# Ten units' second-chunk scores in two column halves, visits to TensorE held open, small VectorE work on ScalarE, and a scheduler with a search

## The chip, the cores and the metric

One Trainium2 chip, one core of it. The metric is the time on the device in microseconds (us) of one execution, as the median of several. Engines are named as in the profile: PE is TensorE (PEld its weight loads), DVE VectorE, ACT ScalarE, POOL GpSimd, SP the engine whose queue issues the DMAs.

## What is computed

A gated linear attention over 4 batches of 8 heads, 768 steps and head size 48, followed by a feed-forward part over all 3072 tokens (384 to 2048 to 384):

```python
scale = np.minimum(mag, 0.999) / (mag + 1e-06)        # mag = |a_re + i a_im|
for t in range(S):
    new_re = ar * S_re - ai * S_im
    new_im = ar * S_im + ai * S_re
    S_re, S_im = new_re + k[t] v[t]^T, new_im
    y[:, :, t] = q[t] . S_re
...
h = x @ w_in                                          # x: y of all heads of a token
g = np.where(h >= 1, h, np.where(h <= -1, 0, (h + 1) ** 2 / 4))
out = g @ w_out
```

All inputs and outputs are fp32.

## The kernel before

**Units.** The work is cut into 12 units `u` of 256 tokens (two chunks `c` of 128), two units side by side in a block; six blocks of 512 tokens go through the feed-forward part. While block `n` is in the feed-forward part, the units of block `n + 1` go through `gates` and `attend`.

**`gates(u)`** loads the gate inputs (`ai`), takes logarithms and angles on ACT, makes running sums of both (units 0 and 1 by matmuls with a triangle, tiles `dec` and `turns`; the others by scans on DVE), rounds the angles to whole turns, and multiplies key and query (`kq`) by growth, cosine and sine on DVE. `spread` moves the products by DMA into head layout, tiles `hd`, 96 rows (real and imaginary of 48) a head.

**`attend(u)`** does for each chunk: `scores` (`sc`: for each of 8 heads a 128 x 128 matrix of keys by queries in fp32, in two groups of four heads, each in one PSUM bank; DVE multiplies it by the causal mask into `am`), `transposes` (`tp`: keys, copied by ACT into `kT`), `values` (`yp`: the state `st` times the queries, plus the masked scores times `V`; ACT copies it to `xr`) and `products` (`dp`: keys by values, which DVE adds to `st`). `values` and `products` use 64 columns of weights at a time and write partitions 0 to 63 and 64 to 127 in turn: here they are called narrow, and scores, transposes and the feed-forward matmuls full. Three PSUM banks `at0` to `at2` are handed round for all of these.

A **visit** is a list of parts that go to PE one behind the other:

```python
if before:                        # values and products of the chunk before
    visit(before + sc[:1])
    visit(sc[1:] + tp)
```

**`moe(blk)`** takes the block through `h` (first product) and `o` (second), each as three float32r matmuls of 512 columns (a high part and a low part of each factor). Between them ACT and DVE make `s`, `g`, `gh`, `gl`. `weights` splits the two weight matrices into high and low parts on DVE and ACT once, in the time of the first block; for the first five it uses PE (`rest`) for the low part.

**The order.** Nothing stands in the order of the code. Each piece is recorded as an operation of a `Plan` with engine, cost in ns, reads, writes and perhaps a due time. `order` works dues backwards through the readers (costs of ACT and DVE times `INFLATE`), then lets each engine in turn take the ready operation with the earliest due. All instructions are emitted in the order of the planned starts, so that each engine's queue follows the plan and only semaphores hold it. A visit's next part was taken at once only if it was ready when the one before was placed; otherwise feed-forward matmuls could come between. `emit` puts idle matmuls (`idle`) where the plan has gaps on PE before the feed-forward part starts.

At the end the flags `fsum`, `fdec`, `wsum` are read, which say whether the fast way holds for these inputs.

Of the kernel before, what the change touches and what calls it, by code (L numbers as in the profile page):

```python
# [28 lines left out]
CH = 128  # L29
U = 256  # L30
# [54 lines left out]
SPLIT_DUE = 3000  # L85

# [38 lines left out]
class Plan:  # L125
# [3 lines left out]
    def __init__(self):  # L129
        self.ops = []  # L130
        self.slots = {}
        self.glued = {}
        self.loose = set()

# [5 lines left out]
    def op(self, eng, cost, fn, r=(), w=(), due=None, dma=0, after=(), glue=None, late=0):  # L140
        i = len(self.ops)
        pre = set(after)
# [26 lines left out]
    def order(self):  # L169
        ops = self.ops  # L170
        n = len(ops)
        succ = [[] for _ in range(n)]
        for i, o in enumerate(ops):
            for p in o[3]:
                succ[p].append(i)
        due = [0.0] * n
        big = 1e12
        for i in range(n - 1, -1, -1):
            eng, cost, _, _, d, dma, late = ops[i]
            t = big if d is None else d  # L180
# [4 lines left out]
            for s in succ[i]:  # L185
                t = min(t, due[s] - own)
            due[i] = t
        left = [len(o[3]) for o in ops]
        ready = [0.0] * n
        end = [0.0] * n  # L190
        start = [0.0] * n
        free = {e: 0.0 for e in ("PE", "DVE", "ACT", "SP", "POOL")}
# [3 lines left out]

        def enable(i):
            heapq.heappush(wait[ops[i][0]], (ready[i], i))

        for i in range(n):  # L200
            if not left[i]:
                enable(i)
        done = 0
        taken = set()
        forced = []
        while done < n:
# [4 lines left out]
            else:  # L211
                best = None
                for e in free:
                    while avail[e] and avail[e][0][1] in taken:
# [9 lines left out]
                    if best is None or t < best[0]:  # L224
                        best = (t, e)
                t, e = best
                while wait[e] and wait[e][0][0] <= t:
# [21 lines left out]
            start[i] = t  # L249
            free[e] = t + cost  # L250
# [10 lines left out]
            for s in succ[i]:  # L261
                left[s] -= 1
                lat = LAT[eng]
                if dma or s in self.loose:
                    lat = 0
                elif ops[s][0] == eng:
                    lat = SAME[eng]
                ready[s] = max(ready[s], end[i] + lat)
                if not left[s]:
                    enable(s)  # L270
            nxt = self.glued.get(i)
            if nxt is not None and not left[nxt]:
                forced.append(nxt)
        self.start, self.end, self.due = start, end, due
        return sorted(range(n), key=lambda i: (start[i], i))
# [46 lines left out]
def gated_scan_moe(  # L322
# [17 lines left out]
    for i, c in enumerate(consts):  # L340
        nc.gpsimd.memset(cst[:, i : i + 1], c)
    c_eps, c_pi2, c_half, c_tiny, c_tin, zero, c_one, c_top = (
# [14 lines left out]

    pl = Plan()
# [5 lines left out]
    def tl(slot, shape, dtype, name, space=None):  # L364
        return pl.tile(
# [203 lines left out]
    def gates(u):  # L569
# [109 lines left out]
        if by_token:  # L679
            D_ = running(A, a, ("o0", "o1"), "dec")  # L680
            for (j0, j1), R in zip(js, D_):
                ve(
                    80,
                    lambda j0=j0, j1=j1, R=R: V_.tensor_copy(
                        state[:, b % 2, 0, j0:j1], R.get()[:, :, U - 1]
                    ),
                    [R],
                    [(STATE[0], j0)],
# [12 lines left out]
        else:  # L701
# [18 lines left out]
            ve(80, lambda: V_.tensor_copy(dst, X0()[:, :, U - 1]), [x0], [STATE[0]])  # L720
# [11 lines left out]
        if by_token:  # L732
            for (j0, j1), R in zip(js, running(I, i, TOKEN[u], "turns")):
                ints = lambda j0=j0, j1=j1: I()[:, j0:j1].bitcast(I32)
                ve(
                    dve((j1 - j0) * U),
                    lambda ints=ints, R=R: V_.tensor_scalar(
                        ints(), R.get(), c, None, op0=ALU.mult
                    ),
                    [R],  # L740
                    [i],
# [41 lines left out]
        if not last:  # L783
            ve(
                80,
                lambda: V_.tensor_scalar_mul(
                    state[:, b % 2, 1], A()[:, :, U - 1], 2 * math.pi
                ),
                [a],
                [STATE[1]],  # L790
# [15 lines left out]
        if u == 1:  # L806
            vt[u] = guest(
                ("o", 4), "V_1", lambda t: t[:, : NC * DM].rearrange("p (c n) -> p c n", c=NC)
            )
        else:  # L810
            vt[u] = tl("V0", [P, NC, DM], F32, f"V_{u}")
        dma(P * NC * DM * 4, lambda t=vt[u]: t.get(), lambda: v[place], w=[vt[u]], late=LATE if u > 1 else 0, eng=LOADS if u > 1 else "SP")
# [100 lines left out]
    def attend(u):  # L913
# [25 lines left out]
        def transposes(c):  # L939
            cs = slice(c * CH, (c + 1) * CH)  # L940
            out = []
            for g in range(2):
# [18 lines left out]
                out.append((4 * 83, run, [hd[h // 3] for h in GROUPS[g]], TP, tail))  # L961
# [3 lines left out]
        def products(c):  # L965
# [4 lines left out]
            ST = tl(turn_of(f"st{b % 2}", 2), [HR, NH, D], F32, f"st_{u}_{c}")  # L970
            carry[b] = ST

            def run():
                for i in range(NH):
                    for a in (0, 64):
# [4 lines left out]
                            V_c[0].get()[:, V_c[1], i * D : (i + 1) * D],  # L980
# [4 lines left out]
            def tail():  # L985
                if old is None:
                    fn = lambda: V_.tensor_copy(ST.get(), DP.get()[:HR])
                else:
                    fn = lambda: V_.tensor_tensor(ST.get(), old.get(), DP.get()[:HR], op=ALU.add)
                pl.op("DVE", dve(DM), fn, r=[DP] + ([old] if old else []), w=[ST])  # L990

            return [(NH * 124, run, [*kT, V_c[0]], DP, tail)]

        def scores(c):
            cs = slice(c * CH, (c + 1) * CH)
            out, ams = [], []
            for g in range(2):
# [649 lines left out]
```

## Time and profile before

| what | value |
|---|---|
| median of 3 runs | 579.27 us (579.22 to 580.12) |
| the profiled execution's own time | 578.85 us |
| its span in the profile | 577.1 us |
| granted TensorE clock | 0.996 |
| PE busy, PEld busy | 562.0, 475.9 us |
| DVE busy, ACT busy | 431.9, 406.9 us |

The span is that of the instructions; 1.75 us of the execution lie around it. Busy times of PE come from modelled ends, and a fp32 matmul shows as two records. Rows in order of time have start and length in us, engine, line, operation, tile written and tiles read, and the number of merged instructions; in brackets the idle time before and what ended it. Rows of groups have busy time, mean ns of one and idle time before. Rows of stretches have, after the stretch and its length, PE, PEld, DVE, ACT and POOL busy us (and counts), the granted clock, the DMA engines' share and GB/s.

### The profile page before, as it was taken

To read this page: it belongs to the slowest core of one execution; us is meant where nothing else is said; L and a number is where in the kernel's file an instruction comes from. 1 tells how busy PE (TensorE), PEld (TensorE's weight loads), DVE (VectorE), ACT (ScalarE), POOL (GpSimd) and SP (SyncE) were. 2 spreads that over 40 slices of the span, in tenths; PEclk is the share of its full clock that TensorE was granted. 3 is DMA by queue.
4 is the path that set the end of the run, shared out by engine and by line. 5 is a ranking of instruction groups with operands and counts; after the bars stand their busy time and mean duration, and the time that the engine had idled before them with its cause. 6 is when DMAs were issued, how large, how long until landed. Compare 5 with 4: busy or idle time off the path is not lost.

```text
span 577.1 us, 9921 instructions
## 1 busy us (share of the span) xinstructions
PE 562.0 (97%) x3888; PEld 475.9 (82%) x3888; DVE 431.9 (75%) x625; ACT 406.9 (71%) x660; POOL 3.3 (1%) x29
## 2 busy tenths in 40 slices
PE   7999999989999999999999999999999999999994
PEld 7788988878888888888888888888888888888883
DVE  4998999989879588579489879788885544455552
ACT  7787899877899998985476666657652333379972
POOL 2000000000000000000000000000000000000000
PEclk9999999999999999999999999999999999999998
DMA  8677443773751623722601612503312200078801
GB/s 352 249 202 253 129 159 109 212 263 121 184 169 43 187 81 111 227 80 73 177 6 40 215 56 82 172 1 90 111 56 72 72 1 8 20 286 292 308 25 61
DMA packets 23142, 77.20 MB, mean 134 GB/s; under 512 B 4336, under 2 KB 9904, under 8 KB 23088
## 3 DMA queue, kind: packets, MB, share of 16 engines
q1 hardware_dynamic: 23088, 76.50, 41.1%
q8 instruction: 32, 0.52, 0.4%
q14 instruction: 22, 0.18, 0.1%
HBM read 51.90 MB, written 4.72 MB: 98 GB/s over the span
## 4 chain that ended last, share of the span: by engine, by line
PE 73%; DVE 12%; ACT 8%; DMA 3%; issue 2%; SPq 0%; ACTq 0%; DVEq 0%
PE o L1302 28%; PE h L1227 28%; PE sc L1004 6%; PE yp L1053 3%; PE yp L1045 3%; DMA raw_o<-in_wl_dram 2%; PE dp L977 2%; ACT ai L608 2%; PE tp L948 2%; ACT x L608 1%; PE px L1138 1%; DMA ai<-in_art_dram 1%; DVE kq L725 1%; DVE kq L834 1%; ACT s L1262 1%
## 5 line engine op out<-in xcount | busy, mean ns | idle before, releaser
L1227 PE MATMUL h<-xH,wi 128*128 128x512 f32 x576 | 180.4, 394 | 0.0
L1302 PE MATMUL o<-gh,wo 128*128 128x512 f32 x576 | 180.1, 394 | 0.0
L1302 PEld LDWEIGHTS o<-gh,wo 128*128 128x128 f32 x576 | 106.3, 188 | 21.8 <-issue 0.7
L1227 PEld LDWEIGHTS h<-xH,wi 128*128 128x128 f32 x576 | 106.1, 188 | 21.1
L1302 PE MATMUL o<-gl,wo 128*128 128x512 f32 x288 | 112.4, 390 | 0.2 <-DVE gl L1289 0.2
L1227 PE MATMUL h<-xL,wi 128*128 128x512 f32 x288 | 112.5, 391 | 0.0
L1271 DVE TENSOR_TENSOR g<-h,s 128x512 f32<-128x512 f32 x96 | 65.8, 685 | 61.0 <-ACT s L1252 42.3
L1252 ACT ACTIVATE s<-h,cst 128x512 f32<-128x512 f32 x96 | 65.6, 685 | 40.4 <-PE h L1227 36.1
L1289 DVE TENSOR_TENSOR gl<-g,gh 128x512 fp32r<-128x512 f32 x96 | 65.9, 687 | 34.5 <-ACT gh L1285 34.4
L1285 ACT CAST gh<-g 128x512 fp32r<-128x512 f32 x96 | 59.1, 615 | 44.6 <-DVE g L1279 44.0
L1302 PEld LDWEIGHTS o<-gl,wo 128*128 128x128 f32 x288 | 54.1, 188 | 12.2 <-DVE gl L1289 0.6
L1227 PEld LDWEIGHTS h<-xL,wi 128*128 128x128 f32 x288 | 54.0, 188 | 12.1 <-DVE xL L1204 0.4
L608 ACT ACTIVATE ai<-ai 128x768 f32<-128x768 f32 x49 | 41.2, 843 | 19.6 <-DVE ai L777 9.2
L1004 PE MATMUL sc<-hd 96*128 96x128 f32 x384 | 49.9, 278 | 0.1
L1004 PEld LDWEIGHTS sc<-hd 96*128 96x128 f32 x384 | 47.1, 191 | 2.8 <-ACT xr L1065 0.5
L1279 DVE SCALAR_TENSOR_TENSOR g<-s,g 128x512 f32<-128x512 f32 x64 | 44.2, 690 | 1.8
L1053 PE MATMUL yp<-am,V 128*64 128x128 f32 x384 | 35.5, 273 | 0.1
L1012 DVE TENSOR_TENSOR am<-sc,sums 128x512 f32<-128x512 f32 x48 | 32.5, 683 | 3.1 <-PE sc L1004 2.9
L1045 PE MATMUL yp<-hd,st 96*64 96x128 f32 x320 | 32.1, 278 | 1.7 <-DVE am L1012 1.6
L402 ACT ACT_TABLE_LOAD x21 | 26.9, 1283 | 0.4
L1045 PEld LDWEIGHTS yp<-hd,st 96*64 96x64 f32 x320 | 19.1, 135 | 8.7 <-issue 4.3
L1053 PEld LDWEIGHTS yp<-am,V 128*64 128x64 f32 x384 | 23.6, 136 | 1.6 <-DVE am L1012 0.5
(111 smaller groups left out, 673.5 us busy)
## 6 DMA issues: line engine op xcount, KB each, us to landing
chk<-in_wl_dram SPq DMA_DIRECT2D x16, 768.0 KB, 5.9
kq<-in_kq_dram SPq DMA_DIRECT2D x12, 768.0 KB, 4.9
ai<-in_ari_dram SPq DMA_DIRECT2D x10, 768.0 KB, 6.5
hd<-x SPq DMA_DIRECT2D x24, 288.0 KB, 4.2
hd<-kq SPq DMA_DIRECT2D x24, 288.0 KB, 5.4
raw_i<-in_wl_dram SPq DMA_DIRECT2D x8, 768.0 KB, 5.6
raw_o<-in_wl_dram SPq DMA_DIRECT2D x8, 768.0 KB, 6.7
V<-in_v_dram SPq DMA_DIRECT2D x12, 384.0 KB, 3.2
```

Source lines behind the costliest of these rows:

```text
L608: lambda: A_.activation(out(), src(), f, **kw),
L1004: PE_.matmul(SC.get()[:, i, :], t[:, 0, cs], t[:, 1, cs], start=True, stop=True)
L1012: lambda: V_.tensor_tensor(AM.get(), SC.get(), mask.unsqueeze(1).to_broadcast([P, 4, CH]), op=ALU.mult,),
L1045: PE_.matmul(o_, st.get().rearrange("p h e -> p (h e)")[:, lo : lo + 64], head(h)[:, 1, cs], start=True, stop=False,)
L1053: PE_.matmul(o_, V.get()[:, c, lo : lo + 64], ams[pr // 2].get()[:, 2 * (pr % 2) + e, :], start=st is None, stop=True,)
L1227: PE_.matmul(H.get(), weight["i", f // 2].get()[:, f % 2, part, sl], x.get()[:, j, :], start=j == 0 and n == 0, stop=j == NJ - 1 and n == 2,)
L1252: lambda: A_.activation(SS.get(), H.get(), AF.Relu, bias=c_half, scale=-0.5 if spare else 0.5),
L1271: lambda: V_.tensor_tensor(G.get(), H.get(), SS.get(), op=ALU.max),
L1279: lambda: V_.scalar_tensor_tensor(G.get(), SS.get(), 1.0, G.get(), op0=ALU.min, op1=ALU.mult),
L1285: pl.op("ACT", act(T), lambda: A_.copy(GH.get(), G.get()), r=[G], w=[GH])
L1289: lambda: V_.tensor_tensor(GL.get(), G.get(), GH.get().bitcast(F32), op=ALU.subtract),
L1302: PE_.matmul(PO[m].get(), weight["o", f // 2].get()[:, f % 2, part, sl], g.get(), start=f == 0 and n == 0, stop=f == NF - 1 and n == 2,)
```

## The change

1. **Scores of chunk 1 of units 2 to 11** (`parted`) are done as narrow matmuls. For two heads, keys 0 to 63 go against all 128 queries, and keys 64 to 127 against the last 64 queries alone (the first 64 lie above the diagonal). The second head of a pair has its two key halves swapped between the partitions, so that neighbours on PE write different halves. Its values come from a swapped copy of `V` that is appended to the load (960 columns instead of 768). DVE masks with a bitwise AND against words of all ones or all zeros (`causal`), since part of the bank isn't written. The banks `at0` to `at2` are allocated once, and cleared by DVE at the start.
2. **Visits.** For these chunks the visit is values, products and both score groups; the transposes are a visit of their own. The planner holds PE open for a visit's next part (`open_`) instead of going on with other work, and adds 140 ns and 212 ns for a change to narrow and back.
3. **Small work goes from DVE to ACT:** the columns of state (`state`, `fdec`), the first state of a batch (`st`) and the rounding of the angles of units 0 and 1 (`ints`). `st` is added to in place, in one buffer.
4. **The scheduler** splits into `first_due`, `forward`, `backward` and `order`: after the first plan it tries 1,000 changed sets of dues and keeps one by the planned end and a falling temperature.

```diff
-            ST = tl(turn_of(f"st{b % 2}", 2), [HR, NH, D], F32, f"st_{u}_{c}")
-            carry[b] = ST
+            ST = carry[b] = old or tl(f"st{b % 2}", [HR, NH, D], F32, f"st_{u}_{c}")
...
+        parted = lambda c: u > 1 and c == 1
...
                 def run(g=g, SC=SC):
-                    for i, h in enumerate(GROUPS[g]):
-                        t = head(h)
-                        PE_.matmul(
-                            SC.get()[:, i, :], t[:, 0, cs], t[:, 1, cs], start=True, stop=True
-                        )
+                    if not parted(c):
+                        for i, h in enumerate(GROUPS[g]):
+                            t = head(h)
+                            PE_.matmul(
+                                SC.get()[:, i, :], t[:, 0, cs], t[:, 1, cs], start=True, stop=True
+                            )
+                        return
+                    for i in (0, 2):
+                        for k in range(2):
+                            for e in (k, 1 - k):
+                                t = head(GROUPS[g][i + e])
+                                a = HALF * (k ^ e)
+                                k0, q0 = c * CH + HALF * k, HALF * k
+                                PE_.matmul(
+                                    SC.get()[a : a + HALF, i + e, q0:],
+                                    t[:, 0, k0 : k0 + HALF],
+                                    t[:, 1, c * CH + q0 : (c + 1) * CH],
+                                    start=True,
+                                    stop=True,
+                                )
...
+                    return V_.tensor_tensor(
+                        pairs(AM),
+                        pairs(SC),
+                        causal.unsqueeze(1).to_broadcast([P, 2, 2, CH]),
+                        op=ALU.bitwise_and,
+                    )
...
-            if before:
+            if before and parted(c):
+                visit(before + sc)
+                if tp:
+                    visit(tp)
+            elif before:
                 visit(before + sc[:1])
                 visit(sc[1:] + tp)
...
-                ve(
-                    dve((j1 - j0) * U),
-                    lambda ints=ints, R=R: V_.tensor_scalar(
-                        ints(), R.get(), c, None, op0=ALU.mult
-                    ),
-                    [R],
-                    [i],
+                pl.op(
+                    "ACT",
+                    act((j1 - j0) * U, psum=True),
+                    lambda ints=ints, R=R: A_.activation(ints(), R.get(), AF.Copy, scale=c),
+                    r=[R],
+                    w=[i],
                 )
...
+    bank_of = {}
+    for i in range(3):
+        bank_of[f"at{i}"] = ps.tile([P, 512], F32, tag=f"at{i}", name=f"at{i}", bufs=1)
+        nc.vector.memset(bank_of[f"at{i}"], 0.0)
...
+                    if e == "PE" and open_ is not None:
+                        if not left[open_]:
+                            t = max(free[e], ready[open_])
+                            if best is None or t < best[0]:
+                                best = (t, e)
+                        continue
...
+            if eng == "PE":
+                if narrow != (i in self.narrow):
+                    narrow = not narrow
+                    cost += TO_NARROW if narrow else TO_WIDE
...
+        for k in range(ROUNDS):
+            part = rng.random()
+            if k == 0 or part < 0.15:
+                share = 1.0 if k == 0 else rng.random()
+                new = [a + (b - a) * share for a, b in zip(due, self.backward(plan))]
+            else:
+                new = list(due)
...
+                for i in rng.sample(near, min(rng.choice((1, 1, 2, 3, 5, 10)), len(near))):
+                    new[i] += rng.gauss(0, shift)
+            trial = self.forward(new)
+            value = max(trial[1])
```

In the changed kernel line numbers are shifted: scores in halves are L1157, full scores L1147, `yp` L1210 and L1218, `dp` L1115, transposes L1087, the feed-forward matmuls L1395 and L1470, the copy of `yp` L1230, the roundings L880. In the lists of instructions that follow, `hd_8_0` is a tile of unit 8, `at0` to `at2` are the shared banks.

Where the order of an engine's instructions is shown, the rows are those of the built program. This is ACT up to the copy of unit 8's first `yp` (`xr`), in the kernel before (`ob` is an output tile, `ai_9` the angles of unit 9):

```order
L1252 ACTIVATE s_3_0_3375<-h_3_0_3314,cst_75 128x512
L402 ACT_TABLE_LOAD
L1329 COPY ob_2_2_3403<-o_2_2_2632 128x512
L608 ACTIVATE ai_9_2443<-ai_9_2443 128x768
L1285 CAST gh_3_0_3408<-g_3_0_3384 128x512
L1065 COPY xr_4_3428<-yp_8_0_0_3386 128x4x128
```

And in the changed kernel:

```order
L1093 COPY kT0_91<-at2_106 128x384
L1093 COPY kT1_92<-at0_102 128x384
L1420 ACTIVATE s_3_0_3355<-h_3_0_3291,cst_75 128x512
L749 ACTIVATE ai_9_2600<-ai_9_2600,cst_75 128x768
L543 ACT_TABLE_LOAD
L1230 COPY xr_4_3395<-at1_104 128x4x128
```

A sine and a table load now stand directly before that copy, where an arctangent and a cast stood.

More of the change, by code (lines that the diff above doesn't have):

```diff
@@ L205, in order @@
         forced = []
+        open_ = None
+        narrow = False
         while done < n:
@@ L260, in order @@
             done += 1
-            for s in succ[i]:
+            for s in self.succ[i]:
                 left[s] -= 1
[L263 to L268, printed above, removed]
-                if not left[s]:
[L270 to L273, printed above, removed]
@@ L274, in order, with backward @@
-        self.start, self.end, self.due = start, end, due
-        return sorted(range(n), key=lambda i: (start[i], i))
+                ready[s] = max(ready[s], end[i] + self.lags[i, s])
+                if not left[s]:
+                    heapq.heappush(wait[ops[s][0]], (ready[s], s))
+            if eng == "PE":
+                open_ = self.glued.get(i)
+        return start, end, took
+    def backward(self, plan):
+        ops = self.ops
+        n = len(ops)
+        start, end, took = plan
+        left = [len(s) for s in self.succ]
+        tail = [0.0] * n
+        free = {e: 0.0 for e in ("PE", "DVE", "ACT", "SP", "POOL")}
+        wait = {e: [] for e in free}
+        avail = {e: [] for e in free}
+        moved = 0.0
+        due = [0.0] * n
+        for i in range(n):
+            if not left[i]:
+                heapq.heappush(wait[ops[i][0]], (0.0, i))
+        for _ in range(n):
+            best = None
+            for e in free:
+                if avail[e]:
+                    t = free[e]
+                elif wait[e]:
+                    t = max(free[e], wait[e][0][0])
+                else:
+                    continue
+                if best is None or t < best[0]:
+                    best = (t, e)
+            t, e = best
+            while wait[e] and wait[e][0][0] <= t:
+                _, i = heapq.heappop(wait[e])
+                heapq.heappush(avail[e], (-start[i], i))
+            _, i = heapq.heappop(avail[e])
+            dma, late = ops[i][5:]
+            if dma:
+                moved = max(tail[i], moved) + dma
+                t = max(moved + DMA_FIX + DMA_END + late, free[e] + took[i])
+                free[e] += took[i]
+            else:
+                t += took[i]
+                free[e] = t
+            due[i] = -t
+            for p in ops[i][3]:
+                left[p] -= 1
+                tail[p] = max(tail[p], t + self.lags[p, i])
+                if not left[p]:
+                    heapq.heappush(wait[ops[p][0]], (tail[p], p))
+        total = max(end)
+        return [total + d for d in due]
@@ new lines, in order @@
+    def order(self):
+        ops = self.ops
+        n = len(ops)
+        self.succ = [[] for _ in range(n)]
+        for i, o in enumerate(ops):
+            for p in o[3]:
+                self.succ[p].append(i)
+        self.lags = {(i, s): self.lag(i, s) for i in range(n) for s in self.succ[i]}
+        due = self.first_due()
+        plan = self.forward(due)
+        best = (max(plan[1]), due, plan)
+        cost = best[0]
+        rng = random.Random(SEED)
+        for k in range(ROUNDS):
[3 more added lines that the diff above has]
+                new = [a + (b - a) * share for a, b in zip(due, self.backward(plan))]
+            else:
+                new = list(due)
+                t = rng.uniform(0, rng.choice(REACH))
+                w = rng.choice((1e3, 5e3, 15e3, 40e3))
+                eng = rng.choice(("DVE", "ACT", "PE", "SP", "DVE", "ACT", None))
+                near = [
+                    i
+                    for i, a in enumerate(plan[0])
+                    if abs(a - t) < w and (eng is None or ops[i][0] == eng)
+                ]
+                shift = rng.choice((500, 2000, 6000, 15000))
+                for i in rng.sample(near, min(rng.choice((1, 1, 2, 3, 5, 10)), len(near))):
+                    new[i] += rng.gauss(0, shift)
+            trial = self.forward(new)
+            value = max(trial[1])
+            heat = 300.0 * (1 - k / ROUNDS) + 6.0
+            if value <= cost or rng.random() < math.exp((cost - value) / heat):
+                cost, due, plan = value, new, trial
+                if cost < best[0]:
+                    best = (cost, due, plan)
+        _, self.due, (self.start, self.end, took) = best
+        for o, t in zip(ops, took):
+            o[1] = t
+        return sorted(range(n), key=lambda i: (self.start[i], i))
```

158 lines of the change are left out of this document (102 added, 56 removed).

## The prediction

> **What bounds the kernel now.** I read the page's span and engine shares first, then busy time in stretches, then TensorE's order of time with the chain of waits, and last the waits.
>
> Of the page, the span and the engines; of the stretches, PE, weight loads, DVE and ACT:
>
> ```profile
> span 577.1 us, 9921 instructions
> PE 562.0 (97%) x3888; PEld 475.9 (82%) x3888; DVE 431.9 (75%) x625; ACT 406.9 (71%) x660; POOL 3.3 (1%) x29
> ...
> 20.00:40.00 20.00, 18.55 (x110) 14.93 (x109) 19.72 (x27) 16.80 (x24) 0.00 (x0) 1.00 0.62 182
> 80.00:100.00 20.00, 20.00 (x153) 17.15 (x152) 19.69 (x26) 19.68 (x32) 0.00 (x0) 1.00 0.25 80
> 120.00:140.00 20.00, 18.36 (x146) 15.68 (x145) 18.55 (x23) 15.56 (x25) 0.00 (x0) 1.00 0.44 168
> 260.00:280.00 20.00, 20.00 (x149) 16.95 (x148) 16.36 (x25) 9.42 (x14) 0.00 (x0) 1.00 0.46 124
> ```
>
> PE is full for all but the start and 120 to 140; from 260 on DVE and ACT have room; at 80 to 100 both are full as well. The granted clock is 1.00 in each. So a microsecond of PE work removed late is a microsecond of the span, and before 140 it is so only if DVE and ACT keep up.
>
> PE in order of time (start, length, line), at the start of attention, at the first matmuls of the feed-forward part (h), at its last group (o) and the last issues of output:
>
> ```profile
> 41.67 1.95 PE L1004 MATMUL sc<-hd 96*128 96x128 f32 x16
> 45.64 1.09 PE L1053 MATMUL yp<-am,V 128*64 128x128 f32 x16
> 48.58 0.84 PE L469 MATMUL rest_o<-raw_o,ident 128*128 128x384 f32 x2
> 49.43 1.05 PE L1004 MATMUL sc<-hd 96*128 96x128 f32 x8
> ...
> 70.33 2.75 PE h L1227 x12
> 563.10 6.13 PE o L1302 x27
> ...
> 568.57 1.68 SPq L392 DMA_DIRECT2D out_dram<-ob  x3
> ```
>
> From 41.67 to 569.2 PE has only the one long hole below. So the time is the first score's start, plus PE's work, plus holes, plus the 7.9 us from 569.2 to the end, in which the last output lands and the flags are read. That execution took 578.85 us around its span of 577.1; the median of the runs is 579.27, 0.42 above it. I sum against 577.1 and carry the difference to the median. I count less than 0.2% (1.2 us) as no change.
>
> **1. Scores in two halves.** Order of time on the chain, with whole runs (two records for one fp32 matmul):
>
> ```profile
> 54.43 0.22 PE yp L1045 x4
> 54.65 0.22 PE yp L1053 x4
> ...
> 456.93 1.79 PE sc L1004 x16
> ...
> 468.89 0.92 PE dp L977 x32
> 469.81 1.09 PE sc L1004 x8
> ```
>
> Eight heads of scores take 1.79 us, so 0.45 for two heads. A pair of 64-column yp matmuls that stand on the two halves of the array takes 0.22 for four records, half of the price of two full ones. The new form needs for two heads one such pair 128 wide (0.22) and one pair 64 wide. That second pair is nearest to dp, 64 columns of weights with 48 moving: 0.92 / 32 x 4 = 0.115. Together 0.335, for a unit 4 x 0.335 = 1.34 in place of 1.79: 0.45 saved, ten units (2 to 11) 4.5 us. Ends: a second pair that costs as much as a wide one (0.22) leaves 0.3 us of gain in all; one at half of yp's price (0.11) gives 4.7. I take 4.5, since dp's shape is nearest. All ten lie in the full stretch.
>
> [...]
>
> Changes between narrow and full matmuls are 24 into narrow and 24 out in both orders, so the count of them saves nothing.
>
> **2. Visits held open.** Unit 8, chunk 1, PE. First before (dp: products of chunk 0; sc: scores, h: feed-forward), then changed (at1 is yp's bank, at2 dp's):
>
> ```order
> L977 MATMUL dp_8_0_3411<-V_8_3246,kT0_84 64x48 x8
> L977 MATMUL dp_8_0_3411<-V_8_3246,kT1_85 64x48 x8
> L1004 MATMUL sc_8_0_1_3432<-hd_8_0_3159 128x128
> L1004 MATMUL sc_8_0_1_3432<-hd_8_1_3166 128x128
> L1004 MATMUL sc_8_0_1_3432<-hd_8_0_3159 128x128
> L1004 MATMUL sc_8_0_1_3432<-hd_8_1_3166 128x128
> L1227 MATMUL h_3_2_3440<-xH_3_2881,wi_1_255 128x512 x2
> ```
>
> ```order
> L1115 MATMUL at2_106<-V_8_3217,kT1_92 64x48 x8
> L1157 MATMUL at0_102<-hd_8_0_3124 64x128
> L1157 MATMUL at0_102<-hd_8_1_3127 64x128
> L1157 MATMUL at0_102<-hd_8_1_3127 64x64
> L1157 MATMUL at0_102<-hd_8_0_3124 64x64
> L1157 MATMUL at0_102<-hd_8_0_3124 64x128
> L1157 MATMUL at0_102<-hd_8_1_3127 64x128
> L1157 MATMUL at0_102<-hd_8_1_3127 64x64
> L1157 MATMUL at0_102<-hd_8_0_3124 64x64
> L1157 MATMUL at1_104<-hd_8_0_3124 64x128
> ```
>
> The second group's scores now follow at once, into at1, yp's bank, which ACT must first have copied out. Before, 14 feed-forward rows stood between. The new wait: after yp, dp (0.92) and the first scores (0.67) run, 1.59 us. The copy and the ACT work that may stand ahead of it:
>
> ```profile
> 184.43 0.39 PE L1053 MATMUL yp<-am,V 128*64 128x128 f32 x4
> 184.75 0.73 PE L1302 MATMUL o<-gh,wo 128*128 128x512 f32 x2
> 185.58 1.28 ACT L402 ACT_TABLE_LOAD   x1
> 186.87 0.59 ACT L1065 COPY xr<-yp 128x512 f32<-128x512 f32 x1
> ...
> 46.78 0.59 ACT L1065 COPY xr<-yp 128x512 f32<-128x512 f32 x1 [0.69 <-PE yp L1053]
> ```
>
> The last of these is a copy for which ACT stood ready: it starts 0.05 after the yp run that is shown above ends (45.64 + 1.09). Copy 0.59 and two hops of 0.05 leave 0.90 of slack. In the row at 186.87 the copy began 2.1 us after yp's last matmuls were through (184.75); nobody waited, now PE would, for 1.2. All that is queued on PE behind it, the feed-forward matmuls with it, waits too. With ACT free it costs nothing; ten visits as late as this one would cost 12. ACT is half idle at 260 to 280, so most visits should find it in time: I take 0.7 (0 to 3).
>
> **3. Small work on ACT, and the start.** DVE, ACT and SP, before, where unit 0's angles are made (L737 rounds them, L834 is the product with the cosine, SP issues moves into head layout), DVE's first work of all, and means of groups on ACT and DVE:
>
> ```profile
> 25.19 0.68 DVE L737 TENSOR_SCALAR ai<-turns 128x512 int32<-128x512 f32 x1
> 26.51 0.41 DVE L737 TENSOR_SCALAR ai<-turns 128x256 int32<-128x256 f32 x1
> 27.48 1.72 ACT L608 ACTIVATE ai<-ai 128x768 f32<-128x768 f32 x2 [0.79 <-DVE ai L745]
> 30.39 0.90 ACT L455 CAST wi<-raw_i 128x768 fp32r<-128x768 f32 x1
> 30.52 1.76 DVE L834 TENSOR_TENSOR x<-kq,ai 128x1536 f32<-128x1536 f32 x1
> 38.05 1.22 SPq L392 DMA_DIRECT2D hd<-kq  x2
> ...
> 6.98 1.83 DVE L622 TENSOR_TENSOR ai<-ai 128x768 f32<-128x768 f32 x2 [6.98 <-DMA ai<-in_art_dram]
> ...
> L695 ACT ACTIVATE x<-dec 128x512 f32<-128x512 f32 x4 | 2.2, 595 | 2.2 <-DVE state L684 1.9 <-PE dec L665 0.4
> L695 ACT ACTIVATE x<-dec 128x256 f32<-128x256 f32 x4 | 1.3, 398 | 0.0
> L1065 ACT COPY xr<-yp 128x512 f32<-128x512 f32 x18 | 10.4, 580 | 4.1 <-PE yp L1053 4.0
> L1065 ACT COPY xr<-yp 128x128 f32<-128x128 f32 x6 | 1.5, 258 | 1.1 <-PE yp L1053 1.1
> L987 DVE COPY st<-dp 96x384 f32<-96x384 f32 x4 | 2.2, 547 | 0.0
> L1012 DVE TENSOR_TENSOR am<-sc,sums 128x512 f32<-128x512 f32 x48 | 32.5, 683 | 3.1 <-PE sc L1004 2.9
> L449 DVE SCALAR_TENSOR_TENSOR raw_o<-raw_o 128x768 uint32<-128x768 uint32 x8 | 7.6, 951 | 0.1
> ```
>
> ACT from unit 0's arctangent to its second sine, before and changed:
>
> ```order
> L608 ACTIVATE ai_0_108<-ai_0_108 128x768
> L608 ACTIVATE ai_1_110<-ai_1_110 128x768
> L455 CAST wi_1_255<-raw_i1_117 128x2x384
> L484 CAST wi_0_214<-rest_i0_1_235 128x384
> L455 CAST wo_0_264<-raw_o0_121 128x2x384
> L484 CAST wi_1_255<-rest_i1_0_270 128x384
> L608 ACTIVATE ai_0_108<-ai_0_108 128x768 x2
> L484 CAST wi_1_255<-rest_i1_1_285 128x384
> L608 ACTIVATE ai_0_108<-ai_0_108,cst_75 128x768
> ```
>
> ```order
> L596 CAST wo_0_280<-raw_o0_132 128x2x384
> L826 COPY state_101<-dec_1_2_232 128x1
> L880 ACTIVATE ai_0_121<-turns_0_0_265 128x512
> L625 CAST wi_1_274<-rest_i1_0_286 128x384
> L880 ACTIVATE ai_0_121<-at2_106 128x256
> L596 CAST wi_2_298<-raw_i2_134 128x2x384
> L749 ACTIVATE ai_0_121<-ai_0_121 128x768
> L928 ACTIVATE state_101<-ai_0_121 128x3
> L625 CAST wi_1_274<-rest_i1_1_294 128x384
> L749 ACTIVATE ai_0_121<-ai_0_121 128x768
> L880 ACTIVATE ai_1_124<-turns_1_0_301 128x512
> L749 ACTIVATE ai_0_121<-ai_0_121,cst_75 128x768
> ```
>
> Ahead of the second sine now stand three roundings (0.595 + 0.398 + 0.595), two state copies (from the two xr rows, 580 at 512 columns and 258 at 128, about 0.15 each) and one weight cast more (0.90): 2.8 us, less the 0.8 that ACT waited for DVE there: +2.0 for the cosine product, L834, at 30.52. What follows takes some back. After the last of unit 0's products seven of its ten moves were still to be issued by SP, now six (one issue, 1.22 / 2 = 0.6). And of the two remainder groups on PE between the first scores and the feed-forward part, one now stands ahead of the scores (0.85 by 48.58 to 49.43). So 2.0 - 0.6 - 0.85 = +0.5 for the first feed-forward matmul. Ends: +3 where nothing is taken back; -1 where DVE, full at 20 to 40 and now relieved of 2.2 us there, brings unit 1's products earlier by that much or half. The masks and cleared banks at the start run in DVE's first 7 us (row at 6.98), before its first load has landed, and cost nothing; without that cover some 2 us, three clears and two masks at about half a microsecond. The mask of chunk 1 becomes an AND on 32-bit words: words in L449 cost 951 / 768 = 1.24 ns an element, the product in L1012 683 / 512 = 1.33, so it stays at 683 and moves nothing. V loads grow by a quarter for ten units; the DMA column of the stretches stands at 0.25 to 0.74: nothing.
>
> **4. The new order.** It is what 1,000 tries made of it; what it can still take is the hole:
>
> ```profile
> PEld yp L1045 <- DVE am L1012: 2.6, 2, 2.1
> 128.84 0.44 PE L1045 MATMUL yp<-hd,st 96*64 96x128 f32 x4 [1.64 <-DVE am L1012]
> ...
> 98.67 0.74 ACT L1262 ACTIVATE s<-s,cst 128x512 f32<-128x512 f32 x1
> ```
>
> Weights wait 2.6 us in all for masked scores on DVE. By then DVE has lost two pairs of roundings (2.2), two first-state copies (1.1) and some state columns, so it is some 3 to 5 us ahead; ACT has as much more, and its row at 98 follows the one before without a gap. I take half of the hole, -1.2 (-2.6 to +2). After 176 there is no hole to take, only one to make.
>
> Sum: -4.5 + 0.7 + 0.5 - 1.2 = -4.5. Span 572.6, that execution 574.35, median 579.27 - 4.5 = 574.8.
>
> **Rivals.**
> A. PE waits for ACT in every held visit. With a lag L of the copy behind yp the wait is L + 0.69 - 1.59 = L - 0.9. L = 2.1 is seen above, L = 0.05 at places with ACT idle. From L = 1.5 on average ten visits cost 6, and the gain is gone (580.8); at 1.8, 583.8. For it: two of the ten copies now stand right behind a table load (1.28); against it: ACT's share late. Chance 0.12, slower.
> B. The half-wide pairs cost as much as wide ones: 579.0 (gain 0.3, other terms even). For it only that 64 x 64 shapes of scores are not in the trace; against it dp. Chance 0.05. C. Loads and matmuls of the new scores stand in series: a wide pair costs twice 0.22 and a half one twice 0.115, for a unit 4 x 0.67 = 2.7 in place of 1.79, 9 us more in ten, 588. For it nothing in the rows; the yp rows, of the same shape, speak against it. Chance 0.01. [...]
> D. The order takes all of the hole and starts earlier: -4.5 - 2.6 - 1.0 = 571.2. For it: DVE, full at 20 to 40, is relieved; against it: ACT's chain above. Chance 0.14.
> E. The start comes +3 late and the hole stays: -4.5 + 3 + 0.7 = 578.5, no change by my bound. Chance 0.08.
>
> **How the numbers follow.** The forecast (572.5 to 577.5) has 0.60, A 0.12, B 0.05, C 0.01, D 0.14, E 0.08. Faster: the forecast, D and a quarter of E, 0.76; same: B and the rest of E, 0.11; slower: A and C, 0.13. The range leaves out A, C and the lower half of D: 571.0 to 579.2.
>
> **What will show it.** New scores: a pair of 128 and a pair of 64 in some 0.34 us. The held visits: no idle PE between the two score groups; else A. First feed-forward matmul near 70.6; the cosine product near 32.5. The hole at 124 to 129 shorter. Wrong would make it an order that PE follows with new waits after 176, or ACT late in the stretch of 80 to 100.

## The result, and the profile after

The changed kernel takes 586.77 us (median of 4 runs, 585.11 to 588.61), the kernel before beside it 579.25: ratio 1.014, 95% interval 1.0113 to 1.0166. It is slower by 7.5 us, where 4.5 us less were forecast. The profiled execution took 585.65 us with a span of 583.9. Of all runs below, one (583.80, with the other seed) counts as slow, being over 1.5% above the fastest of its kernel, and is left out of its ratio.

Page: the span and the engines.

```profile
span 583.9 us, 10317 instructions
PE 562.8 (96%) x4058; PEld 474.2 (81%) x4058; DVE 429.0 (73%) x600; ACT 413.4 (71%) x690; POOL 4.3 (1%) x33
```

PE is as busy as before (562.0) and 6.8 us of span are new: idle time came in, more than work went out. In order of time on PE, the first scores, the first feed-forward matmuls (h), the last (o):

```profile
42.84 1.95 PE L1147 MATMUL at<-hd 96*128 96x128 f32 x16
71.53 0.70 PE L1395 MATMUL h<-xH,wi 128*128 128x512 f32 x2
575.64 0.39 PE L1470 MATMUL o<-gl,wo 128*128 128x512 f32 x1
575.96 0.09 PEld L1578 LDWEIGHTS at<-ok,cst 128*1 128x1 f32 x2 [0.35 <-issue]
```

The first scores come 1.17 later than before (41.67), the feed-forward part 1.4 (70.09 by the start of its first matmul), PE's last work 6.8 (569.15). What follows takes 7.9 us as before. So most was lost between. Busy time in stretches, of after; the first numbers are PE, weight loads, DVE and ACT, and then the granted clock:

```profile
100.00:120.00 20.00, 17.24 (x131) 14.30 (x130) 16.65 (x26) 16.35 (x28) 0.00 (x0) 0.99 0.63 211
120.00:140.00 20.00, 20.00 (x173) 17.21 (x173) 19.52 (x25) 17.21 (x25) 0.00 (x0) 0.93 0.39 136
140.00:160.00 20.00, 17.39 (x125) 13.75 (x125) 13.94 (x21) 11.71 (x20) 0.00 (x0) 1.00 0.71 226
160.00:180.00 20.00, 19.05 (x164) 15.49 (x164) 16.70 (x25) 19.43 (x34) 0.00 (x0) 1.00 0.25 76
```

In the first, third and fourth of these PE lacks 2.8, 2.6 and 1.0 us. The telling part is the other two columns: at 140 to 160 ACT is busy 11.7 of 20 and DVE 13.9, less than before (16.2 and 18.5 in the same stretch). No engine is full there; all wait for each other. The waits at 68 to 180 (engine, line, what it waited for: us, times, longest):

```profile
ACT gh L1453 <- PE o L1470: 10.9, 3, 5.2
DVE gl L1457 <- ACT gh L1453: 9.2, 3, 4.1
...
PEld h L1395 <- DVE g L1439: 3.5, 2, 3.2
PE h L1395 <- DVE g L1439: 2.8, 1, 2.8
...
PE o L1470 <- ACT wo L596: 1.3, 1, 1.3
PE o L1470 <- DVE wo L601: 1.3, 1, 1.3
```

The first line does not occur in the kernel before. ACT's cast of the gate product (gh) waits for o matmuls of PE, which come later than it in a step's flow. The place, on ACT, DVE and PE:

```profile
106.49 0.19 ACT L749 ACTIVATION_READ_ACCUMULATOR x<-ai 128x1 f32 x1
110.20 0.62 ACT L1453 CAST gh<-g 128x512 fp32r<-128x512 f32 x1 [3.52 <-PE o L1470]
110.73 0.93 ACT L749 ACTIVATE ai<-ai,cst 128x768 f32<-128x768 f32 x1
...
110.86 0.69 DVE L1457 TENSOR_TENSOR gl<-g,gh 128x512 fp32r<-128x512 f32 x1 [3.18 <-ACT gh L1453]
...
109.55 0.62 PE L1470 MATMUL o<-gh,wo 128*128 128x512 f32 x2
117.91 0.73 PE L1395 MATMUL h<-xH,wi 128*128 128x512 f32 x2 [2.76 <-DVE g L1439]
```

ACT stands from 106.7 to 110.2, until PE has run o matmuls that start at 109.55; behind gh stand an angle of the attention part (L749) and all that follows; DVE stands behind gl, which reads gh. Eight us later the backlog reaches PE: 2.76 us idle for a gate product of DVE. The chain of waits names another cause for the angle at 110.73, a transfer:

```profile
108.52 2.21 DMA hd<-x
110.73 0.94 ACT ai L749
...
hd<-x SPq DMA_DIRECT2D x2, 32.0 KB, 5.1
```

The last line, of the DMA issues at 104 to 112 (KB each, median us from issue to landing), speaks against it: issued at 108.52, it lands near 113.6, after the angle has begun. The chain cuts the transfer off there; the rows of the engine itself show that ACT was stopped by gh.

At 150.12 gh waits 5.19 and at 158.93 another 2.17 in the same way, and PE follows with waits of 1.3 for weights that ACT and DVE should have split by then.

The code says why gh waits. gh and gl have six buffers in turn, three steps' worth, and LAG is 3: gh of step k overwrites what the o matmuls of step k - 3 read. In moe's loop gemm1(k), which creates gh of step k, is written down before gemm2(k - 3), which creates that reader. The plan collects the users of a buffer at the time its successor is created, so it does not know of this reader, and the order that it makes is free to put gh ahead of it on ACT. The wait is on the chip all the same (3.52, 5.19 and 2.17 us above). This is a reading of the code so far; the experiments test it.

### The profile page after: what moved, and what is told of

Same layout as the page of the kernel before. It is cut to its first block, busy times and chain, and to the rows that moved or that the text cites. A ratio compares the mean times of both kernels' runs of the same rounds, so it can differ in the third digit from the quotient of the medians.

```text
span 583.9 us, 10317 instructions
## 1 busy us (share of the span) xinstructions
PE 562.8 (96%) x4058; PEld 474.2 (81%) x4058; DVE 429.0 (73%) x600; ACT 413.4 (71%) x690; POOL 4.3 (1%) x33
## 4 chain that ended last, share of the span: by engine, by line
PE 77%; ACT 8%; DVE 6%; DMA 4%; SPq 2%; issue 1%; ACTq 0%; DVEq 0%
PE h L1395 31%; PE o L1470 29%; PE at L1210 3%; PE at L1218 3%; PE at L1115 2%; ACT ai L749 2%; SPq L533 2%; PE at L1157 2%; PE at L1147 2%; DMA hd<-x 2%; PE at L1087 2%; ACT x L749 1%; DMA ai<-in_art_dram 1%; PE at L1306 1%; DMA raw_o<-in_wl_dram 1%
## 5 line engine op out<-in xcount | busy, mean ns | idle before, releaser
L1395 PE MATMUL h<-xH,wi 128*128 128x512 f32 x576 | 182.0, 397 | 2.8 <-DVE g L1439 2.8
L1470 PE MATMUL o<-gh,wo 128*128 128x512 f32 x576 | 179.5, 392 | 2.7 <-ACT wo L596 1.3
L1470 PEld LDWEIGHTS o<-gh,wo 128*128 128x128 f32 x576 | 107.0, 188 | 25.7 <-ACT wo L596 1.7
L1395 PEld LDWEIGHTS h<-xH,wi 128*128 128x128 f32 x576 | 106.0, 189 | 25.6 <-DVE g L1439 3.7
L1470 PE MATMUL o<-gl,wo 128*128 128x512 f32 x288 | 112.6, 391 | 0.9 <-DVE gl L1457 0.9
L1395 PE MATMUL h<-xL,wi 128*128 128x512 f32 x288 | 112.8, 392 | 0.4 <-DVE xL L1372 0.4
L1470 PEld LDWEIGHTS o<-gl,wo 128*128 128x128 f32 x288 | 54.0, 188 | 13.6 <-DVE gl L1457 2.2
L1395 PEld LDWEIGHTS h<-xL,wi 128*128 128x128 f32 x288 | 54.2, 188 | 12.6 <-DVE xL L1372 0.8
L749 ACT ACTIVATE ai<-ai 128x768 f32<-128x768 f32 x49 | 41.3, 844 | 7.8 <-DVE ai L918 4.2
L1218 PE MATMUL at<-am,V 128*64 128x128 f32 x352 | 32.8, 273 | 0.0
L1210 PE MATMUL at<-hd,st 96*64 96x128 f32 x304 | 30.5, 278 | 0.0
L1525 PE MATMUL idle<-sums,ident 128*128 128x128 f32 x178 | 24.3, 294 | 1.8 <-POOL sums masks.py:66 1.8
L1525 PEld LDWEIGHTS idle<-sums,ident 128*128 128x128 f32 x178 | 23.7, 210 | 2.7 <-POOL sums masks.py:66 1.8
L1147 PEld LDWEIGHTS at<-hd 96*128 96x128 f32 x192 | 24.0, 198 | 0.9
L1147 PE MATMUL at<-hd 96*128 96x128 f32 x192 | 24.4, 282 | 0.0
L1430 ACT ACTIVATE s<-s,cst 128x512 f32<-128x512 f32 x32 | 23.1, 722 | 0.6
```

The lines of the kernel that those rows point to most:

```text
L749: lambda: A_.activation(out(), src(), f, **kw),
L1147: PE_.matmul(SC.get()[:, i, :], t[:, 0, cs], t[:, 1, cs], start=True, stop=True)
L1210: PE_.matmul(o_, st.get().rearrange("p h e -> p (h e)")[:, lo : lo + 64], head(h)[:, 1, cs], start=True, stop=False,)
L1218: PE_.matmul(o_, V.get()[:, vo : vo + 64], ams[pr // 2].get()[:, 2 * (pr % 2) + e, :], start=st is None, stop=True,)
L1395: PE_.matmul(H.get(), weight["i", f // 2].get()[:, f % 2, part, sl], x.get()[:, j, :], start=j == 0 and n == 0, stop=j == NJ - 1 and n == 2,)
L1470: PE_.matmul(PO[m].get(), weight["o", f // 2].get()[:, f % 2, part, sl], g.get(), start=f == 0 and n == 0, stop=f == NF - 1 and n == 2,)
```

## The experiments

Theories, as they arose. T1: 1,000 tries fit an order too closely to the plan's durations. T2: the small work makes ACT late. T3: visits held open make PE wait. T4: half scores make holes wherever the rest is. T5: luck of one order. T6: the missing wait between gh and the o matmuls. The first four experiments were set up before T6 was found, the next four beside T4 and T5; two of those gave no time. The kernel before has medians of 577.98 to 579.05 us in the four groups of runs; each ratio is against its own group.

**No tries.** The plan's first order.

```
-    ROUNDS, SEED = 1000, 0
+    ROUNDS, SEED = 0, 0
```

> The changed kernel with the first plan taken as it is: no priority shift is tried (held visits, mode costs, half scores and the small work on ScalarE stay). Theory T1, the search fits the order to the planner's own durations and the in-order queues then stall on the chip at 105 to 175 us: the holes on PE there, 11.3 us in the changed kernel against 3.1 before, go back to 3 to 5, time 577 to 580. Theory T2, the small work overloads ScalarE: holes stay, 585 to 588. Theory T3, holding visits open makes the holes: they stay too, 585 to 588.

585.61 us, ratio 1.0108 (1.0078 to 1.0138). As slow as with tries within their intervals, so T1 doesn't have its 577 to 580. But the loss lies elsewhere. The planner itself, run from the kept kernels, lets this first plan end at 575.26 us and the one that the tries kept at 568.56: most of the slowness was planned, and the run doesn't test T1 as it was meant to. Its trace is of a run of 582.87, below the median. Its waits at 160 to 180:

```profile
PEld at L1157 <- ACT xr L1230: 3.4, 1, 3.4
PE at L1157 <- ACT xr L1230: 3.3, 1, 3.3
```

That is rival A, once, in a held visit; ACT gh never waits for PE o in this kernel.

**Half scores alone.** The kernel before with the new score tiles (small work on DVE, old planner: its `order` and its weights of a visit).

```
-    def order(self): ... forward(), backward(), tries ...
+    def order(self): ... as before ...
-    pl.op("ACT", 120, lambda: A_.copy(...
+    ve(80, lambda: V_.tensor_copy(...
```

> The kernel before with the half scores alone (their visits, masks, the appended values and the fixed banks; planner and small work as before). All theories: the ten visits are 0.45 us shorter, 4.5 us in all, holes as before, 574 to 576. If the fixed banks or the masks cost something of their own: above 577.

579.48 us, ratio 1.0007 (0.9991 to 1.0023). The half scores gain nothing under the old planner, and the 574 to 576 expected are missed. PE's order of time has 34 stretches of narrow matmuls in place of 24, as the second group's scores become a piece of their own. That this is the reason, and not the banks or the masks, is not shown by this run; the one without held visits, below, bears on it.

**The new planner alone.** Full scores, small work on DVE, tries.

```
-        parted = lambda c: u > 1 and c == 1
+        parted = lambda c: False
-    pl.op("ACT", 120, lambda: A_.copy(...
+    ve(80, lambda: V_.tensor_copy(...
```

> The kernel before with the new planner alone (held visits, mode costs, 1,000 shifts; full scores, small work on VectorE). T1: 584 to 590, holes between 75 and 180 us of 8 to 12 us. T2: 578 to 580. T3: 584 to 590 as well, so that the first run tells T1 from T3.

577.62 us, ratio 0.9985 (0.9972 to 0.9998). T1 and T3 in their first form fall: the tries make an order that is slightly better, with holes of PE of 1.1 us in all from 60 us on.

**The changed kernel with the old planner.**

```
-    def order(self): ... forward(), backward(), tries ...
+    def order(self): ... as before ...
```

> The changed kernel with the planner of before (its rule for parts of a visit, its costs, no search): half scores and small work on ScalarE stay. T1: 575 to 577, the first feed-forward matmul 0 to 2 us later than before, holes of 3 to 5 us. T2: 583 to 588. T3: 575 to 577.

581.90 us, ratio 1.0058 (1.0036 to 1.0080), outside the ranges of all three theories. It is 2.4 above half scores alone, which points to the small work on ACT, less than T2 asked; the old planner itself puts 2.5 between the two (its plans end at 568.51 and 566.05).

**Small work back on DVE; and full scores with the small work on ACT.** Both keep the new planner and its tries.

```
-    pl.op("ACT", act((j1 - j0) * U, psum=True), lambda ...: A_.activation(ints(), R.get(), AF.Copy, scale=c), ...
+    ve(dve((j1 - j0) * U), lambda ...: V_.tensor_scalar(ints(), R.get(), c, None, op0=ALU.mult), ...
```

> The changed kernel with the small work (roundings from the decode, state columns, two copies of 48 columns) back on DVE; half scores, held visits and the 1,000 tries stay. T2 (ACT with the small work on it is late at the start and at 100 to 170, and PE waits there): 572 to 576, first feed-forward matmul back near 70, holes after it under 4 us. T4 (any order for half scores has more holes than the planner sees, wherever the small work is): 579 to 585, holes of 8 us or more.

```
-        parted = lambda c: u > 1 and c == 1
+        parted = lambda c: False
```

> The changed kernel with full scores of chunk 1 in all units (no half scores); small work on ACT, new planner and tries stay. T2: 580 to 585 (2 to 6 above the kernel that has the new planner alone, 577.6), with the first feed-forward matmul near 71.5. T4 (half scores make the holes): 577 to 579.

576.35 us, ratio 0.9966 (0.9954 to 0.9979), and 579.05 us, ratio 1.0015 (0.9994 to 1.0036). The first lies just above T2's range. Taken alone it looked like proof of T2: 10 us for one part. The second spoke against it: the same work on ACT with full scores costs 1.4 us (against 577.62). And T2 has no reason why ACT should idle 8 of 20 us. What the kernels differ in is the wait that T6 names: ACT gh for PE o from 68 to 560 is 16.4 us in 6 in the changed kernel, 3.1 in 1 and 1.5 in 2 in these two. An order meets it or doesn't.

**Two variants without a time.** The changed kernel with another seed (T2 expected 584 to 588, T5 576 to 583) and with only the roundings back on DVE (T2: 574 to 578, or 583 to 588 if the small copies are at fault) deadlock: instructions of their orders wait for each other in a ring, so there is no program to time. What the two programs stop at is the wait of T6. On ACT the cast of gh, of step 6 in the one and of step 9 in the other, both in the first block, waits for its buffer to come free, and what stands behind it never starts.

**The wait made known to the plan.** Two calls change places; buffers, engines, tries and seed stay.

```
         for k in range(NF + LAG):
-            if k < NF:
-                gemm1(k)
             if k >= LAG:
                 gemm2(k - LAG)
+            if k < NF:
+                gemm1(k)
```

> The changed kernel with two calls swapped in moe's loop: gemm2(k - LAG) is written down before gemm1(k), so that the plan knows that the rounded gate products gh and gl of step k (6 buffers, three steps' worth) overwrite what gemm2(k - 3) reads. T6 (the tries found orders that only look short because that wait was missing in the plan; ACT then stands at gh until PE's o matmuls are through, and all behind it on ACT is late): 572 to 578, waits of ACT gh on PE o under 2 us in all at 68 to 180 instead of 10.9, holes on PE after the first feed-forward matmul under 4 us instead of 12. T2 (the small work makes ACT late): 581 to 587, holes of 6 us or more.

575.65 us, ratio 0.9954 (0.9936 to 0.9972): 11 us off, with everything else of the change in it. The page, the stretches and the largest waits at 68 to 180 of this kernel:

```profile
span 573.6 us, 10284 instructions
PE 559.6 (98%) x4056; PEld 473.0 (82%) x4056; DVE 428.9 (75%) x600; ACT 410.5 (72%) x690; POOL 4.3 (1%) x33
```

```profile
100.00:120.00 20.00, 20.00 (x149) 16.96 (x148) 19.60 (x30) 19.58 (x32) 0.00 (x0) 1.00 0.84 256
...
140.00:160.00 20.00, 20.00 (x141) 16.97 (x141) 18.24 (x28) 18.87 (x34) 0.00 (x0) 1.00 0.63 195
```

```profile
ACT s L1420 <- PE h L1395: 3.6, 1, 3.6
ACT gh L1453 <- DVE g L1439: 3.0, 2, 2.0
```

PE is full in both stretches, ACT and DVE work 18 to 20 of 20 there, and gh waits only for its own input. The busy time of ACT over the span is nearly the same (410.5 and 413.4). T6 holds. The order itself shows it at the same place:

```profile
104.39 0.60 ACT L1453 CAST gh<-g 128x512 fp32r<-128x512 f32 x1
104.90 0.84 ACT L749 ACTIVATE ai<-ai 128x768 f32<-128x768 f32 x1
105.77 0.85 ACT L749 ACTIVATE x<-ai 128x768 f32<-128x768 f32 x1
106.53 0.18 ACT L749 ACTIVATION_READ_ACCUMULATOR x<-ai 128x1 f32 x1
106.74 0.94 ACT L749 ACTIVATE ai<-ai,cst 128x768 f32<-128x768 f32 x1
```

After the read of the accumulator comes the angle at once, which stood behind gh before.

One swap also makes another order, so T5 has to be ruled out. The planner is part of each kernel and gives its plan without the chip. Compared with the rule that a buffer's next writer starts after its last reader, its list of waits lacks, among all the buffers that it hands out, only those of the six of gh and gl; with the two calls swapped it lacks none. In the plan of the changed kernel 8 casts of gh start before the last reader of their buffer has ended, by 16.0 us in all. The first is the one shown above: it is planned for 104.8, its buffer's last reader until 108.4. The kernels with the small work on DVE, with full scores, and with the new planner alone have 2 such casts each; the kernel before, the one without tries and the two with the old planner have none.

| kernel | casts ahead of a reader | plan ends, as it is and swapped | median, as it is and swapped |
|---|---|---|---|
| changed | 8 | 568.56, 568.82 | 586.77, 575.65 |
| small work on DVE | 2 | 567.22, 567.35 | 576.35, 575.38 |
| full scores | 2 | 572.31, 572.63 | 579.05, 578.39 |

The swap is worth 11.1, 1.0 and 0.7 us, and by the plans it should cost a little each time. The medians lie 5.8 to 10.4 us behind the planned ends in all kernels with the new planner, but 18.2 in the changed one. (The swapped ones of the lower rows follow.)

**Another seed, the small work on DVE, and the kernel before, each with the two calls swapped.**

```
-    ROUNDS, SEED = 1000, 0
+    ROUNDS, SEED = 1000, 1
```

> The same with another seed of the 1,000 tries. T6: within 1.5 us of the kernel before it in this list, 572 to 578. T5 (an order's luck decides): more than 3 us away from it.

577.71 us, ratio 0.9982 (0.9956 to 1.0009). That is 2.1 from the other seed, or 1.4 by the 577.06 that is the median without the 583.80: about T6's bound of 1.5, less than T5's 3. Its runs spread wide, from 574.42 to 583.80. The trace is of the longest and says nothing of the others; in it DVE stands 4.1 us once for a weight that lands late, and PE's weight loads wait 3.1 for ACT's copy of yp. This seed, which deadlocks without the swap, runs with it.

> The same two calls swapped, and the small work back on DVE (half scores, held visits and tries stay). T6: within 2 us of the kernel with the small work on ACT, 572 to 577; the 10 us that the move to ACT cost without the swap are gone. T2: 5 us or more faster than with the small work on ACT.

575.38 us, ratio 0.9959 (0.9941 to 0.9977): the engine of the small work makes no difference once the wait is known. T2 falls as an explanation of the loss.

> The kernel before with only the two calls swapped, nothing of the change. T6: 577 to 579.5, since gh waits little there (its one long hole, at 124, is put down to masked scores): the missing wait was there already and did no harm in that order. If the missing wait cost the kernel before as much: below 575.

578.28 us, ratio 0.9999 (0.9978 to 1.0020). The wait was unknown to the plan of the kernel before as well, and its order happened not to meet it: the swap leaves that plan as it was, start for start, so the two times are those of one order.

**Full scores, and visits not held open, both with the two calls swapped.**

```
-        parted = lambda c: u > 1 and c == 1
+        parted = lambda c: False
```

> The changed kernel with the two calls swapped (the plan knows the reuse of gh and gl) and full scores of chunk 1 in all units. It prices the half scores in an order that keeps to its plan: the half scores' 4.5 us by the prediction's first term would put it at 579 to 581 against 575.65 with half scores; if the half scores are worth nothing in the end: 575 to 576.5.

578.39 us, ratio 1.0009 (0.9990 to 1.0029): the half scores are worth 0.55% between the ratios 1.0009 and 0.9954, 3.2 us, or 2.7 by the medians. Neither end that was written down; nearer to the first. Each is one order, and another seed alone moved the time by 1.4 to 2.1, so the size is rough.

```
-            if before and parted(c):
-                visit(before + sc)
-                if tp:
-                    visit(tp)
-            elif before:
+            if before:
```

> The changed kernel with the two calls swapped and the visits not held open (the second group's scores are a piece of their own again, which the plan may put elsewhere). If holding them costs waits for ACT's copy: 573 to 575. If not holding them costs ten more changes between narrow and full matmuls, as in the kernel with half scores alone (34 in place of 24, some 0.3 us each): 577 to 579. Else within 1 us of 575.65.

577.43 us, ratio 0.9988 (0.9975 to 1.0000): held visits are worth some 1.8 us of that, with the same reserve, and PE's order of time has 34 narrow stretches again, as the second range (577 to 579) supposed.

## Why the prediction was wrong

The forecast was on the wrong side, 7.5 us slower in place of 4.5 faster. Step by step:

1. **Half scores: right in mechanism and in price of the matmuls.** Of after's chain of waits, two visits and what follows the second:

```profile
85.53 0.92 PE at L1115 x32
86.45 1.54 PE at L1157 x32
87.99 4.31 PE h L1395 x18
...
132.43 0.92 PE at L1115 x32
133.35 1.35 PE at L1157 x32
134.71 2.28 PE h L1395 x9
```

A unit's scores take 1.35 as worked out (1.34). Rivals B and C are out: with loads and matmuls in series C had 2.7 us for a unit, and the trace has 32 records, all on the same 96 rows, in 1.35. In the end the half scores bring 2.7 to 3.2 us (swapped calls, with and without), where terms 1 and 2 together had 3.8.

2. **Held visits: right.** Of the nine visits that the chain holds, seven take 1.35, one 1.47 and one 1.54, and PE never waits for the copy in the changed kernel (0.7 forecast). Rival A came about elsewhere: PE waits 3.6 us in all without tries, 4.3 in the longest run of the other seed, 1.1 or less in the others. (Its 580.8 and 583.8 set the wait on top of a sum that already holds 0.7 for it; 580.1 and 583.1 would be right.) What the prediction left out is that holding visits open spares changes: it said 24 into narrow in both orders "so the count of them saves nothing". Without holding there are 34. In the changed kernel's chain a change costs about 0.15 one way and 0.24 back: the four yp records at 102.54 take 0.37 where the next four take 0.22, and the nine of h at 134.71 take 2.28 where nine at 95.74 take 2.04.

3. **Small work on ACT, and the start: mis-sized.** The feed-forward part starts 1.4 later, not 0.5. The term that failed is the 0.85 for the remainder group: from the first scores to the first feed-forward matmul PE takes 28.7 us, and 28.4 before, so nothing was taken back there. The three clears take 0.485 each and the two instructions for the masks 0.21 and 0.80, all by 4.1, before DVE's first work on an angle at 5.91. The cosine product was placed well (32.5 forecast):

```profile
L973 DVE TENSOR_TENSOR x<-kq,ai x12: 1745/1753/1760, 32.2 to 429.9; 128x1536 f32<-128x1536 f32 x12
```

4. **The new order: the step that failed.** Where the prediction had a gain, 6.9 us of idle PE and lowered clock came in. It took -1.2 with +2 as its worst, and named as the stock "what it can still take is the hole". It looked at the old order's holes as all that a new one could draw on, and at engine load for what it might add. It did not ask which waits the planner knows. A planner that is free to try 1,000 orders moves work to where its model is blind; the casts of gh went ahead of their buffers' last readers. In the stretches 60 to 200 the engine PE lacks 2.0 us before and 7.3 after (140 less the busy times):

```profile
60.00:80.00 20.00, 19.08 (x189) 17.15 (x186) 19.47 (x28) 17.18 (x31) 0.00 (x0) 1.00 0.57 184
80.00:100.00 20.00, 20.00 (x170) 16.89 (x170) 19.93 (x26) 19.86 (x33) 0.00 (x0) 1.00 0.27 94
...
180.00:200.00 20.00, 19.94 (x124) 16.38 (x121) 13.51 (x19) 18.27 (x28) 0.00 (x0) 1.00 0.57 147
```

(the four between stand above). With the 1.6 us that the clock took after one hole (below), +6.9. So the 6.8 us later end of PE is +1.4 of start, +6.9 here, and a rest of -1.5: the half scores' gain of about 3, less 0.9 in which PE is idle at 200 to 300 and 0.6 of loss not accounted for. The sentence that after 176 there was no hole to take, "only one to make", held for the stretch ahead of 176 too: 10.9 of the 16.4 us of gh's waits lie there, where ACT and DVE are needed; the 5.5 us later on cost PE little (the 0.9 at 200 to 300, nothing after).

One reading of the old trace was also off: the hole at 124 to 129 was put down to masked scores, which PE's row names. DVE's row shows what they stood behind:

```profile
124.77 0.56 DVE L431 TENSOR_SCALAR y_o<-raw_o 128x768 uint32<-128x768 uint32 x1 [1.46 <-DMA raw_o<-in_wl_dram]
```

DVE waited for a weight that landed late, and the mask at 128.09 was queued behind it and four more rows. The weight was issued at 117.64 and took 7.1 to land; that less work on DVE brings it earlier is not shown. Nor was there 2.6 to gain: that is the wait of the weight loads, and PE itself is idle 1.64 there (the row at 128.84).

What stays open: a part of the time without tries. Of the 10.0 us between it (585.61) and the swapped kernel (575.65), 6.4 are in the plans (575.26 and 568.82). For the rest there are the held visit's wait of 3.3 and a granted clock of 0.985 to 0.992 in the five runs from 585.59 up, against 0.994 or 0.995 in the three below; that was not taken apart. Swapping the two calls brings the change near what was forecast: 575.65 and, with the small work on DVE, 575.38, faster than the kernel before by 0.46% and 0.41%, 2.4 to 2.7 us of the 4.5.

## What to carry to other kernels

When a planner or search sets the order, list the waits that the chip enforces and check that the plan has each: here a buffer's reader, written down after the buffer's next writer, was missing, and cost 11 us of 587 while no engine was full. Compare the planned end with the time, too: an order that lies 18 us behind its plan where others lie 6 to 10 has met something that the plan doesn't hold. A line in the waits where an engine stands for work that comes *later* in the flow (a cast for a matmul that consumes casts) was here a buffer's reuse, not a slow engine: its 16.4 us are not among the waits with the two calls swapped, while ACT is nearly as busy (410.5 and 413.4). And price an effect of engine choice in more than one order before believing it: the same move cost 10 us in one order, 1.4 in a second and about none in a third.

## What the hardware showed that was not expected

A hole on PE cost more than its length here: 2.76 us idle, and 1.6 more in the work behind it. Granted clock (the column behind POOL's) around the hole of 2.76 us, in after:

```profile
116.00:118.00 2.00, 0.09 (x1) 0.09 (x1) 2.00 (x4) 1.97 (x5) 0.00 (x0) 1.00 0.96 378
118.00:120.00 2.00, 2.00 (x13) 1.86 (x14) 2.00 (x4) 2.00 (x4) 0.00 (x0) 0.87 1.02 399
120.00:122.00 2.00, 2.00 (x10) 1.90 (x10) 2.00 (x4) 1.97 (x3) 0.00 (x0) 0.50 0.96 341
122.00:124.00 2.00, 2.00 (x9) 1.60 (x8) 2.00 (x3) 1.44 (x3) 0.00 (x0) 0.78 0.56 226
```

and what ran there, of the chain of waits:

```profile
118.88 2.74 PE at L1147 x16
121.62 3.41 PE h L1395 x12
```

In this trace half clock comes after work has begun again. The 16 score records take 2.74 where 1.79 is the price, the 12 of h 3.41 where 2.78 is (first h of this kernel): 1.6 us more. The holes of 1.3 us at 153 and 154.8 left the clock at 1.00; the ones of 2.95 (other seed) and 3.28 us (no tries) brought it to 0.50 and, as the mean of 4 us, 0.66 in the stretches behind them. In between, the length alone doesn't decide: of two holes of 1.88, the one that ends at 401.85 with the small work on DVE left the clock at 1.00, and the one in the kernel before with the two calls swapped did not:

```profile
129.00 0.44 PE L1045 MATMUL yp<-hd,st 96*64 96x128 f32 x4 [1.88 <-DVE am L1012]
130.00:132.00 2.00, 2.00 (x25) 2.00 (x24) 2.00 (x4) 1.97 (x3) 0.00 (x0) 0.50 0.00 0
```

In these traces 2.76 was enough, and once 1.88. No limit in length follows from these runs.
